# A gated recurrence with a capacity-limited mixture of experts: router logits made pair by pair, softmax sums moved to PSUM, and a new order of work

## The chip, the core and the metric

The kernel runs on one core of a Trainium2 chip. The core has five engines that work side by side, each through its own instructions in the order written: TensorE (PE, with its weight loads shown apart as PEld), VectorE (DVE), ScalarE (ACT), GpSimd (POOL) and SyncE (SP), which here only issues DMA transfers. They wait for each other through semaphores. The metric is the device time of one execution in microseconds; of several runs the median is given.

## What is computed

`x`, `r_gate` and `i_gate` are 4 x 5056 x 256 in float32, 20.7 MB each. The first part is a recurrence over time, the second a mixture of eight experts on its output, where each expert takes only its 80 best tokens:

```python
sig_r, sig_i = sigmoid(r_gate), sigmoid(i_gate)
a_t   = exp(8 * sig_r * log(clip(sigmoid(a_param), 1e-6, 1 - 1e-6)))
x_in  = sqrt(maximum(1 - a_t * a_t, 1e-6)) * sig_i * x
h     = a_t[:, t] * h + x_in[:, t]           # for each t; y[:, t] = h
# the 20224 tokens of y, 256 wide, go on:
logits = y @ w_gate                          # 8 experts
expert = argmax(logits); gate = softmax(logits)[expert]
for e in range(8):                           # 80 tokens at most, by gate
    out[tok] = gate[tok] * (relu(y[tok] @ w1[e]) @ w2[e])   # w1 256x1024, w2 1024x256
# every other row of out is zero
```

So nearly all 20.7 MB of the output are zeros, which the kernel writes by DMA ("zero fills"), and 640 rows are written over them at the end.

## The kernel before

**Tiles.** All 20224 tokens stay on the chip, transposed: `Y` has 25 slots of 128 partitions x 2 halves of the 256 features x 1024 tokens. Slots 0 to 19 end up with the recurrence's states of the 20 "pairs" (stretches of 1024 tokens, the last one 768). The inputs of later pairs pass through slots that are still free, slots 20 to 24 above all. A "unit" is a pair or a part of one: pair 0 is units 0 and 1, pair 19 units 20 and 21.

**Work of a unit**, each step one letter of the table `ORDER`: `r`, `i`, `x` load the inputs (SP, L108); `T` and `I` are the two tanh on ACT (L116, L135); `A` transposes r to PSUM tile `pr` on PE (L122), `E` makes the decay from it on ACT (L124), half by half; `Q` squares it on POOL (L127); `S` takes square roots of several units in one batch on ACT (L131), with a table load on either side; `U` is the product with x on POOL (L138); `B` transposes it to `pu` on PE (L145, L146); `N` is the normalisation on DVE (L149) and `Y` the scan on DVE (L159).

**The router.** Tokens are gated in six "chains": four of 4 pairs, one of 2, and one of the last 1792 tokens. A chain has nine stages, `c0.0` to `c5.8`. Stage 0 makes the logits of the whole chain on PE (L227), 32 float32 matmuls, each two passes in the trace, into one PSUM bank `pl`. Stage 1 copies them out (DVE, L234), 2 turns them (PE, L237, into PSUM bank `pt`), 3 subtracts the maximum (DVE, L241, L242), 4 is the exponential (ACT, L244), 5 finds the first maximum (DVE, L248 to L250), 6 divides by the sum (DVE, L253 to L256; L254 adds 1e-9 to the sums, a tensor_scalar from SBUF to SBUF), 7 turns back (PE, L258) and 8 stores (DVE, L261). In the last chain `l19` and `l20` make the logits of units 19 and 20, and `c5.0` those of unit 21.

**What sets the order.** `ORDER` is a fixed table of such letters, and each engine gets its instructions in that order. `Z` issues one zero fill of 256 tokens (256 KB, in runs of 1 KB, L206) on SP's queue. The fills that are left are written in the program behind the first eight weight loads (`load_w1`, `load_w2` for experts 0 and 1, L295, L298), which reuse slots 20 to 23; some of them are put further ahead in SP's queue by the scheduler.

**After the order**: the choice of 80 tokens per expert (L366 to L438), the gathering of their columns (L509, L510), the matmuls (L524 `ph`, L526 `po`; behind each half of an expert's matmuls the weights of the expert after next are loaded), and the writing of the rows (L537).

Of the kernel before, what the change touches and what calls it, by code (L numbers as in the profile page):

```python
# [63 lines left out]
def moe_kernel(ctx, tc, x, r_gate, i_gate, a_param, w_gate, w1, w2, out, capacity=80):  # L64
# [16 lines left out]
    nc.scalar.dma_start(ap, a_param.rearrange("(h p) -> p h", p=P))  # L81
# [41 lines left out]
    def decay(u, h):  # L123
        nc.scalar.activation(state(u, h), prs.pop((u, h))[:, :UNITS[u][2]], AF.Exp, scale=L[:, h:h + 1], bias=L[:, h:h + 1])  # L124
# [45 lines left out]
    nc.vector.memset(zero, 0.0)  # L170
# [46 lines left out]
    def logits(s, p0, p1, o, n):  # L217

        if 'pl' not in st: st['pl'] = ps_g.tile([P, 512], F32, name="pl")
        c0 = (p0 - CHAINS[s][0]) * PC + o // NR  # L220
        pl = st['pl']
        m = (p1 - p0) * (n // NR)
        for b in range(4):
            for h in range(2):
                for j in range(4):
                    src = Y[:, p0:p1, h, o + 4 * j + b:o + n:NR] if p1 - p0 > 1 else Y[:, p0, h, o + 4 * j + b:o + n:NR]
# [3 lines left out]
    def r_logits(s, n):  # L230
        if s < len(CHAINS) - 1: logits(s, *CHAINS[s], 0, C)
        else: logits(s, UNITS[LASTU][0], UNITS[LASTU][0] + 1, *UNITS[LASTU][1:])
    def r_copy(s, n):
        nc.vector.tensor_copy(lg[:, :count(s)], st['pl'][:, :count(s)])  # L234
    def r_turn(s, n):
        pt = st['pt'] = ps_g.tile([P, 512], F32, name="pt")
        for k in range(nblk(s)): nc.tensor.transpose(pt[:n, k * P:k * P + P], lg[:, k * P:k * P + n], ident)  # L237
    def part(t, s, n, c0=0): return t[:n, c0:c0 + P * nblk(s)].rearrange("p (m e) -> p m e", e=E)
    def r_max(s, n):
        lv = part(st['pt'], s, n)  # L240
# [372 lines left out]
```

## Time and profile before

| | |
|---|---|
| median of 3 runs | 327.68 us (323.89 to 328.71) |
| the profiled execution, and its span | 327.59 us, 325.86 us |
| busy: PE, PEld, DVE, ACT, POOL | 239.6, 201.8, 218.2, 220.8, 202.4 us |
| moved by DMA | 100.77 MB, 309 GB/s over the span |
| chain of waits, largest lines | DVE L159 12%, PE L227 11%, DVE L149 7%, PE L122 7% |

The profile gives for each instruction when it started and how long it took, and, where an engine stood idle before it, for how long and what ended the idle time. Ends of matmuls are modelled, so the sum of their durations says less than the distance from one burst to the next. The chain of waits is followed back from the last instruction to whatever released each step. Stages by time: the ordered part runs to about 246 us, the choice of tokens to 262, the experts to the end.

### The profile page before, as it was taken

Reading aid. Unit: us, or ns where it says so; the run is one execution under the profiler, and the core shown is the slowest. Engines: PE = TensorE matmul, PEld = TensorE weight load, DVE = VectorE, ACT = ScalarE, POOL = GpSimd, SP = SyncE. Lnnn points to the kernel's source line nnn. Section 1 sums busy time; section 2 is a strip of 40 time slices with the busy share of each in tenths; the row PEclk is TensorE's granted clock in tenths of the full one; section 3 lists DMA queues with packets and bytes.
Section 4 is the critical chain, followed back from the end, with each engine's and each line's share of the span. In section 5 each row is a group of like instructions: output and inputs, shape, how many; then the busy total and the mean of one; then the engine's idle time right before and its main releaser. Section 6 shows DMA issues by size and latency. Waiting matters only on the chain.

```text
span 325.9 us, 6481 instructions
## 1 busy us (share of the span) xinstructions
PE 239.6 (74%) x2044; PEld 201.8 (62%) x2044; DVE 218.2 (67%) x467; ACT 220.8 (68%) x399; POOL 202.4 (62%) x289
## 2 busy tenths in 40 slices
PE   0556498689764998676994996394625688999993
PEld 0345498664763757676474935274414478999992
DVE  1000459994999949999769569998718657566420
ACT  4999979999886949999769769547002365445400
POOL 2239998999795957989747570925003466563612
PEclk9999879999998799997999699676575789999999
DMA  6999999999999899979949998909999404999941
GB/s 230 409 412 410 410 355 367 415 406 412 380 383 292 325 362 322 406 257 396 325 161 335 344 315 335 333 20 368 331 363 376 160 2 164 332 339 345 333 111 28
DMA packets 51673, 100.77 MB, mean 309 GB/s; under 512 B 3504, under 2 KB 32048, under 8 KB 51632
## 3 DMA queue, kind: packets, MB, share of 16 engines
q1 hardware_dynamic: 50976, 99.63, 85.1%
q0 software_dynamic: 384, 0.66, 0.6%
q8 instruction: 18, 0.29, 0.4%
q14 instruction: 23, 0.19, 0.2%
q10 hardware_dynamic: 272, 0.00, 0.0%
HBM read 78.91 MB, written 21.36 MB: 308 GB/s over the span
## 4 chain that ended last, share of the span: by engine, by line
PE 31%; DVE 28%; issue 14%; ACT 10%; POOL 8%; DMA 5%; POOLq 3%; DVEq 0%; ACTq 0%; SPq 0%
DVE Y L159 12%; PE pl L227 11%; DVE pu L149 7%; PE pr L122 7%; PE pu L145 6%; PE pu L146 6%; POOL Y L510 6%; ACT Y L124 4%; ACT Y L131 3%; DVE Y L254 3%; POOLq L503 2%; DMA Y<-in_r_gate_dram 2%; ACT Y L116 1%; DMA tiny<-in_a_param_dram 1%; DMA Y<-in_x_dram 1%
## 5 line engine op out<-in xcount | busy, mean ns | idle before, releaser
L138 POOL TENSOR_TENSOR Y<-Y 128x2048 f32<-128x2048 f32 (+2 forms) x22 | 90.5, 4119 | 18.1 <-ACT Y L135 8.2
L127 POOL TENSOR_TENSOR Y<-Y 128x2048 f32<-128x2048 f32 (+2 forms) x22 | 71.6, 3253 | 41.7 <-ACT Y L124 36.6
L145 PE MATMUL pu<-ident,Y 128*128 128x128 f32 x316 | 83.0, 302 | 19.5 <-DVE Y L159 14.8
L159 DVE TENSOR_TENSOR_SCAN Y<-Y,pu 128x1024 f32<-128x1024 f32 (+8 forms) x50 | 93.2, 1882 | 0.9
L146 PE MATMUL pu<-ident,Y 128*128 128x128 f32 x316 | 81.7, 298 | 1.4 <-POOL Y L138 1.4
L122 PE MATMUL pr<-ident,Y 128*128 128x128 f32 x316 | 52.2, 316 | 33.9 <-ACT Y L124 18.5
L149 DVE SCALAR_TENSOR_TENSOR pu<-Y,pu 128x1024 f32<-128x1024 f32 (+2 forms) x44 | 48.6, 1109 | 42.1 <-ACT Y L131 28.4
L122 PEld LDWEIGHTS pr<-ident,Y 128*128 128x128 f32 x316 | 42.5, 164 | 40.9 <-ACT Y L124 22.9
L145 PEld LDWEIGHTS pu<-ident,Y 128*128 128x128 f32 x316 | 49.4, 156 | 26.4 <-DVE Y L159 15.1
L124 ACT ACTIVATE Y<-pr,tiny 128x1024 f32<-128x1024 f32 (+2 forms) x44 | 49.0, 1115 | 23.0 <-PE pr L122 22.9
L146 PEld LDWEIGHTS pu<-ident,Y 128*128 128x128 f32 x316 | 49.5, 157 | 1.7 <-POOL Y L138 1.7
L526 PE MATMUL po<-Y,rows 128*80 128x128 f32 x256 | 46.5, 274 | 0.0
L524 PE MATMUL ph<-Y 128*128 128x80 f32 x256 | 42.7, 258 | 2.4 <-DVE Y L510 1.4
L116 ACT ACTIVATE Y<-Y 128x2048 f32<-128x2048 f32 (+2 forms) x22 | 38.0, 1730 | 5.9 <-DMA Y<-in_r_gate_dram 5.9
L227 PE MATMUL pl<-Y 128*32 128x256 f32 (+4 forms) x512 | 35.7, 443 | 5.9 <-issue 3.8
L524 PEld LDWEIGHTS ph<-Y 128*128 128x128 f32 x256 | 37.5, 191 | 2.9 <-issue 2.9
L135 ACT ACTIVATE Y<-Y 128x2048 f32<-128x2048 f32 (+2 forms) x22 | 38.0, 1730 | 1.7 <-DMA Y<-in_i_gate_dram 1.6
L131 ACT ACTIVATE Y<-Y 128x2048 f32<-128x2048 f32 (+2 forms) x22 | 37.0, 1731 | 2.5 <-POOL Y L127 2.4
L509 ACT COPY Y<-Y 128x2 f32 x224 | 22.9, 191 | 18.1 <-issue 15.4
L510 POOL COPY Y<-Y 128x2 f32 x192 | 24.5, 200 | 15.5 <-issue 8.6
L227 PEld LDWEIGHTS pl<-Y 128*32 128x32 f32 x512 | 15.0, 131 | 23.8 <-issue 20.4
L526 PEld LDWEIGHTS po<-Y,rows 128*80 128x80 f32 x256 | 28.5, 152 | 0.0
(124 smaller groups left out, 178.1 us busy)
## 6 DMA issues: line engine op xcount, KB each, us to landing
out_dram<-Y SPq DMA_DIRECT2D x79, 256.0 KB, 5.9
Y<-in_r_gate_dram SPq DMA_DIRECT2D x18, 1024.0 KB, 7.9
Y<-in_i_gate_dram SPq DMA_DIRECT2D x18, 1024.0 KB, 10.9
Y<-in_x_dram SPq DMA_DIRECT2D x18, 1024.0 KB, 10.6
Y<-in_moe_w_dram SPq DMA_DIRECT2D x32, 512.0 KB, 5.1
Y<-in_r_gate_dram SPq DMA_DIRECT2D x3, 512.0 KB, 4.0
Y<-in_i_gate_dram SPq DMA_DIRECT2D x3, 512.0 KB, 9.3
Y<-in_x_dram SPq DMA_DIRECT2D x3, 512.0 KB
```

What stands on the lines that cost most here:

```text
L122: nc.tensor.transpose(pr[:, c0:min(n, g + 512):nb], rr[:, at:at + P], ident)
L124: nc.scalar.activation(state(u, h), prs.pop((u, h))[:, :UNITS[u][2]], AF.Exp, scale=L[:, h:h + 1], bias=L[:, h:h + 1])
L127: nc.gpsimd.tensor_tensor(halves('r', u), a, a, op=ALU.mult)
L131: nc.scalar.activation(q, q, AF.Sqrt, scale=-0.25, bias=0.25)
L138: nc.gpsimd.tensor_tensor(i, i, flat('x', u), op=ALU.mult)
L145: nc.tensor.matmul(cols, xx[:, at:at + P], ident, start=True, stop=False, is_transpose=True)
L146: nc.tensor.matmul(cols, ii[:, at:at + P], ident, start=False, stop=True, is_transpose=True)
L149: nc.vector.scalar_tensor_tensor(pu, halves('r', u)[:, h], 0.5e-3, pu, op0=ALU.max, op1=ALU.mult)
L159: nc.vector.tensor_tensor_scan(y[:, s0:s1], y[:, s0:s1], q[:, s0:s1], init, op0=ALU.mult, op1=ALU.add)
L227: nc.tensor.matmul(pl[32 * j:32 * j + 32, c0:c0 + m], gates(h, b), src, start=(b == 0 and h == 0), stop=(b == 3 and h == 1), tile_position ...
L524: nc.tensor.matmul(ph[:, c % (FC // 2)], w1v(e1)[:, h, c * P:c * P + P], XG[:, e1, h], start=(h == 0), stop=(h == 1))
L526: nc.tensor.matmul(po[:, h, :P], h2T[:, c], w2v(e2)[:, c, h * P:h * P + P], start=(c == 0), stop=(c == FC - 1))
```

## The change

1. Logits are made one pair at a time: a letter `l` with the unit's number takes the place of stage 0, so that 32 matmuls of 64 columns are issued per pair instead of 32 of 256 per chain. They go to one of two halves of one bank `pl`, even chains to the first and odd ones to the second. `pt` becomes one lasting tile.
2. The exponential is written to `lg` in SBUF, the keys of the first maximum to `pt`, and the sums, with their addition of 1e-9, to `pt` in PSUM; the turn back goes to `pt` too, so that `pl` is free after its copy.
3. `a_param` is loaded by SP as its first transfer, where ACT's queue did it beside SP's first loads.
4. `Z` issues one fill of 512 tokens (512 KB) in runs of 4 KB, from a zeroed 128 x 1024 piece of slot 19, as long as no decay of pair 19 has been written there; after that it issues two old fills.
5. `ORDER` is a new table: other places for loads, fills, chain stages and root batches (12 instead of 11).

```diff
 ORDER = """
-r0@20 r1@20 i0@21 r2@22 i1@21 T0 r3@23 w T1 A0.0 E0.0 r4@24 I0 A0.1 E0.1 T2 Q0 A1.0 i2@18 E1.0 I1 Z ...
+r0@20 r1@20 i0@21 r2@22 i1@21 T0 x0@23 w A0.0 r3@24 E0.0 T1 A0.1 E0.1 i2@18 I0 Q0 A1.0 E1.0 T2 A1.1 ...
...
-    nc.scalar.dma_start(ap, a_param.rearrange("(h p) -> p h", p=P))
+    nc.sync.dma_start(ap, a_param.rearrange("(h p) -> p h", p=P))
...
     def decay(u, h):
+        if UNITS[u][0] == PAIRS - 1: st['last'] = True
...
-    nc.vector.memset(zero, 0.0)
+    nc.vector.memset(Y[:, PAIRS - 1, 0], 0.0)
...
-    def zero_fill(k):
+    def zero_fill(k, wide=False):
...
+            if wide and N - a >= 512 and not st.get('last'):
+                nz[0] = a + 512
+                nc.sync.dma_start(out[a:a + 512].rearrange("(p b) d -> p (b d)", p=P), Y[:, PAIRS - 1, 0])
+                continue
+            if wide:
+                zero_fill(2)
+                continue
...
-    def logits(s, p0, p1, o, n):
-        if 'pl' not in st: st['pl'] = ps_g.tile([P, 512], F32, name="pl")
+    pl = ps_g.tile([P, 2, 256], F32, name="pl")
+    pt = ps_g.tile([P, 512], F32, name="pt")
+    def logits(u):
+        p, o, n = UNITS[u]
+        if p < 18: o, n = 0, C
...
-                    nc.tensor.matmul(pl[32 * j:32 * j + 32, c0:c0 + m], gates(h, b), src,
+                    nc.tensor.matmul(pl[32 * j:32 * j + 32, s % 2, c0:c0 + n // NR], gates(h, b), Y[:, p, h, o + 4 * j + b:o + n:NR],
...
-        nc.scalar.activation(part(st['pt'], s, n, 2 * P), part(st['pt'], s, n), AF.Exp)
+        nc.scalar.activation(part(lg, s, n), part(pt, s, n), AF.Exp)
...
-        m = NR * nblk(s); key = part(st['pl'], s, n, 2 * P)
+        m = NR * nblk(s); key = part(pt, s, n, 2 * P)
...
-        total = sm[:n, :NR * nblk(s)]
-        nc.vector.tensor_reduce(out=total, in_=part(st['pt'], s, n, 2 * P), op=ALU.add, axis=AX.X)
+        total = pt[:n, :NR * nblk(s)]
+        nc.vector.tensor_reduce(out=total, in_=part(lg, s, n), op=ALU.add, axis=AX.X)
         nc.vector.tensor_scalar_add(total, total, 1e-9)
-        nc.vector.reciprocal(total, total)
+        nc.vector.reciprocal(sm[:n, :NR * nblk(s)], total)
```

The order on three pieces, before and in the change. Line numbers of the change stand up to nine higher for the same step.

PE at the first logits (numbers behind a tile's name tell tiles of one name apart), before:

```order
L146 MATMUL pu_513<-ident_72,Y_70 128x128
L122 MATMUL pr_538<-ident_72,Y_70 128x128 [waits Activation_49]
L122 MATMUL pr_538<-ident_72,Y_70 128x128 x7
L227 MATMUL pl_547<-Y_70 32x256 x32
L145 MATMUL pu_589<-ident_72,Y_70 128x128 [waits DMAHW7_49,DVE_49,PE_49]
L146 MATMUL pu_589<-ident_72,Y_70 128x128 [waits DMAHW5_49,Pool_49]
```

and in the change:

```order
L146 MATMUL pu_369<-ident_72,Y_70 128x128
L147 MATMUL pu_369<-ident_72,Y_70 128x128
L236 MATMUL pl_109<-Y_70 32x64 x32
L146 MATMUL pu_423<-ident_72,Y_70 128x128 [waits DVE_49]
L147 MATMUL pu_423<-ident_72,Y_70 128x128
```

The burst of 32 matmuls that stood behind the states of four pairs is a quarter as wide and serves one pair; the next three bursts of the chain stand further down, between other transposes.

SP from the load of unit 20's x to the expert weights, before:

```order
L108 DMA Y<-in_x_dram 128x1024
L206 DMA out_dram<-Y 256x1x256
L112 DMA Y<-in_i_gate_dram 128x512
L206 DMA out_dram<-Y 256x1x256 x3
L112 DMA Y<-in_x_dram 128x512
L206 DMA out_dram<-Y 256x1x256 x11
L295 DMA Y<-in_moe_w_dram 128x2x512 x4
L298 DMA Y<-in_moe_w_dram 128x4x256 x4
L206 DMA out_dram<-Y 256x1x256 x15
```

and in the change:

```order
L112 DMA Y<-in_i_gate_dram 128x512
L108 DMA Y<-in_x_dram 128x1024
L112 DMA Y<-in_x_dram 128x512
L214 DMA out_dram<-Y 256x1x256 x26
L300 DMA Y<-in_moe_w_dram 128x2x512 x4
L303 DMA Y<-in_moe_w_dram 128x4x256 x4
L214 DMA out_dram<-Y 256x1x256 x30
```

Ahead of this piece SP's queue has 49 fills of 256 KB before, and 11 of 512 KB and one of 256 KB in the change. Behind the load of the last x come 26 fills before and 56 in the change.

PE at the end of the router, before:

```order
L258 MATMUL pl<-ident,lg 128x128 [waits DVE_49]
L227 MATMUL pl<-Y 32x64 [waits DVE_49]
L227 MATMUL pl<-Y 32x64 x31
L227 MATMUL pl<-Y 32x32 x32
L227 MATMUL pl<-Y 32x16 x4
L227 MATMUL pl<-Y 32x16 [waits DVE_49]
L227 MATMUL pl<-Y 32x16 x27
L237 MATMUL pt<-ident,lg 112x128 [waits DVE_49]
L258 MATMUL pl<-ident,lg 128x112 [waits DVE_49]
```

and in the change:

```order
L236 MATMUL pl<-Y 32x32 x32
L236 MATMUL pl<-Y 32x16 [waits DVE_49]
L236 MATMUL pl<-Y 32x16 x3
L236 MATMUL pl<-Y 32x16 [waits DVE_49]
L236 MATMUL pl<-Y 32x16 x27
L263 MATMUL pt<-ident,lg 128x128 [waits DVE_49]
L242 MATMUL pt<-ident,lg 112x128 [waits DVE_49,Activation_49]
L263 MATMUL pt<-ident,lg 128x112 [waits DVE_49]
```

Unit 19's logits have moved ahead of the last transposes, and chain 4's turn back (the 128x128 one) now comes behind the last logits instead of ahead of unit 19's.

## Rows read from the trace of the kernel before

**Rows 1.** Busy time by window: PE, PEld, DVE, ACT, POOL, clock, DMA share, GB/s.

```profile
0.00:218.00 218.00, 160.07 (x1248) 128.93 (x1249) 157.02 (x149) 182.67 (x132) 158.45 (x62) 0.92 0.92 340
218.00:234.00 16.00, 8.22 (x40) 6.20 (x38) 14.12 (x22) 7.22 (x10) 4.81 (x4) 0.65 0.97 323
234.00:246.00 12.00, 4.56 (x194) 3.84 (x194) 3.45 (x12) 0.25 (x1) 0.29 (x1) 0.64 1.04 351
```

**Rows 2.** Groups by line and shape, 0 to 246 us: busy, mean ns | idle before.

```profile
L227 PE MATMUL pl<-Y 128*32 128x256 f32 x256 | 28.3, 607 | 0.0
...
L227 PE MATMUL pl<-Y 128*32 128x64 f32 x64 | 2.0, 291 | 1.1 <-DVE rows L261 1.1
...
L227 PE MATMUL pl<-Y 128*32 128x16 f32 x64 | 1.0, 194 | 3.8 <-issue 3.8
```

**Rows 3.** Timeline of DVE: start, duration, [idle before <- what ended it].

```profile
79.65 0.42 DVE L234 COPY lg<-pl 128x256 f32<-128x256 f32 x1 [2.71 <-PE pl L227]
...
118.90 0.42 DVE L234 COPY lg<-pl 128x256 f32<-128x256 f32 x1 [4.34 <-PE pl L227]
...
165.97 1.23 DVE L149 SCALAR_TENSOR_TENSOR pu<-Y,pu 128x1024 f32<-128x1024 f32 x1 [3.24 <-PE pu L146]
...
194.94 0.42 DVE L234 COPY lg<-pl 128x256 f32<-128x256 f32 x1 [2.76 <-PE pl L227]
```

**Rows 4.** Timeline of ACT, behind three bursts of logits.

```profile
119.90 1.21 ACT L124 ACTIVATE Y<-pr,tiny 128x1024 f32<-128x1024 f32 x1 [4.42 <-PE pr L122]
...
166.78 1.21 ACT L124 ACTIVATE Y<-pr,tiny 128x1024 f32<-128x1024 f32 x1 [2.73 <-PE pr L122]
...
219.31 0.56 ACT L124 ACTIVATE Y<-pr,tiny 128x256 f32<-128x256 f32 x1 [4.05 <-PE pr L122]
```

**Rows 5.** Chain of waits: start, length, what; the pieces on L254.

```profile
97.98 3.65 DVE Y L254
...
148.44 1.18 DVE Y L254
...
204.65 3.05 DVE Y L254
```

**Rows 6.** Who waited for whom, 60 to 234 us: total, times, longest.

```profile
PEld pl L258 <- DVE lg L256: 9.3, 4, 3.2
...
ACT Y L116 <- DMA Y<-in_r_gate_dram: 5.9, 5, 3.0
```

**Rows 7.** Timeline of all engines near the start.

```profile
0.81 0.87 SPq L108 DMA_DIRECT2D Y<-in_r_gate_dram  x2
...
5.59 0.17 DVE L87 TENSOR_SCALAR tiny<-tiny 128x2 f32<-128x2 f32 x1 [4.26 <-DMA tiny<-in_a_param_dram]
...
7.54 2.00 ACT L116 ACTIVATE Y<-Y 128x1024 f32<-128x1024 f32 x2
...
26.73 1.90 ACT L135 ACTIVATE Y<-Y 128x2048 f32<-128x2048 f32 x1
```

**Rows 8.** DMA issues of 0 to 9 us: count, KB each, median us to landing.

```profile
Y<-in_r_gate_dram SPq DMA_DIRECT2D x2, 512.0 KB, 4.3
```

**Rows 9.** Groups of the whole span: the table loads around root batches.

```profile
L131 ACT ACT_TABLE_LOAD x11 | 14.1, 1283 | 0.2
```

**Rows 10.** Timeline of the end of the router.

```profile
241.74 0.27 DVE L234 COPY lg<-pl 128x112 f32<-128x112 f32 x1 [6.96 <-PE pl L227]
...
244.75 0.18 DVE L254 TENSOR_SCALAR Y<-Y 112x16 f32<-112x16 f32 x1
```

**Rows 11.** Timeline of SP's queue, from the load of unit 20's x.

```profile
218.25 0.33 SPq L108 DMA_DIRECT2D Y<-in_x_dram  x1
...
239.34 14.93 SPq L206 DMA_DIRECT2D out_dram<-Y  x15
268.10 6.77 SPq L295 DMA_DIRECT2D Y<-in_moe_w_dram  x3
```

**Rows 12.** Timeline of PE, where the third expert's matmuls begin.

```profile
277.76 0.35 PE L524 MATMUL ph<-Y 128*128 128x80 f32 x2
```

More of the change, by code (lines that the diff above doesn't have):

```diff
@@ L50 @@
+B19.0 I20 E20.0 t B19.1 S19.1 A20.1 x20@21 l18 x21@21 Z Z Z Z E20.1 T21 Q20 N19.0 Z A21.0 E21.0 N19.1 I21 Z A21.1 U20 E21.1 Y19.0 Z Q21
+S20.2 Z Y19.1 B20.0 U21 Z N20.0 B20.1 Z c4.1 Y20.0 l19 Z N20.1 B21.0 Y20.1 c4.2 Z N21.0 B21.1 c4.3 Z l20 N21.1 c4.4 Y21.0 Y21.1 c4.5 l21
+c4.6 c4.7 c5.1 c4.8 c5.2 c5.3 c5.4 c5.5 c5.6 c5.7 c5.8
 """
@@ L216, in gates @@
     def gates(h, b): return wg[:, h, 24 - E * b:56 - E * b]
-    def logits(s, p0, p1, o, n):
-        if 'pl' not in st: st['pl'] = ps_g.tile([P, 512], F32, name="pl")
-        c0 = (p0 - CHAINS[s][0]) * PC + o // NR
-        pl = st['pl']
-        m = (p1 - p0) * (n // NR)
+    pl = ps_g.tile([P, 2, 256], F32, name="pl")
[3 more added lines that the diff above has]
+        if p < 18: o, n = 0, C
+        s = next(k for k, c in enumerate(CHAINS) if p < c[1])
+        c0 = (p - CHAINS[s][0]) * PC + o // NR
         for b in range(4):
@@ L225, in logits @@
                 for j in range(4):
[L226 to L227 removed]
+                    nc.tensor.matmul(pl[32 * j:32 * j + 32, s % 2, c0:c0 + n // NR], gates(h, b), Y[:, p, h, o + 4 * j + b:o + n:NR],
                                      start=(b == 0 and h == 0), stop=(b == 3 and h == 1), tile_position=(0, 32 * j))
     def by_expert(v, n, s): return v[:n, :NR * nblk(s)].unsqueeze(2).broadcast_to([n, NR * nblk(s), E])
[L230 to L232 removed]
     def r_copy(s, n):
[L234 removed]
+        nc.vector.tensor_copy(lg[:, :count(s)], pl[:, s % 2, :count(s)])
     def r_turn(s, n):
[L236 removed]
         for k in range(nblk(s)): nc.tensor.transpose(pt[:n, k * P:k * P + P], lg[:, k * P:k * P + n], ident)
@@ L239, in r_max @@
     def r_max(s, n):
-        lv = part(st['pt'], s, n)
+        lv = part(pt, s, n)
         nc.vector.tensor_reduce(out=mx[:n, :NR * nblk(s)], in_=lv, op=ALU.max, axis=AX.X)
@@ L251, in r_gate_ @@
     def r_gate_(s, n):
-        total = sm[:n, :NR * nblk(s)]
-        nc.vector.tensor_reduce(out=total, in_=part(st['pt'], s, n, 2 * P), op=ALU.add, axis=AX.X)
+        total = pt[:n, :NR * nblk(s)]
+        nc.vector.tensor_reduce(out=total, in_=part(lg, s, n), op=ALU.add, axis=AX.X)
         nc.vector.tensor_scalar_add(total, total, 1e-9)
-        nc.vector.reciprocal(total, total)
-        nc.vector.tensor_tensor(part(lg, s, n, 2 * P), part(st['pl'], s, n, 2 * P), by_expert(sm, n, s), op=ALU.mult)
+        nc.vector.reciprocal(sm[:n, :NR * nblk(s)], total)
+        nc.vector.tensor_tensor(part(lg, s, n, 2 * P), part(pt, s, n, 2 * P), by_expert(sm, n, s), op=ALU.mult)
     def r_back(s, n):
-        for k in range(nblk(s)): nc.tensor.transpose(st['pl'][:, k * P:k * P + n], lg[:n, (2 + k) * P:(3 + k) * P], ident[:n, :n])
+        for k in range(nblk(s)): nc.tensor.transpose(pt[:, k * P:k * P + n], lg[:n, (2 + k) * P:(3 + k) * P], ident[:n, :n])
     def r_store(s, n):
         c0 = CHAINS[s][0] * PC + (K1 if s >= EARLY else 0)
-        nc.vector.tensor_copy(rows[:, c0:c0 + count(s)], st.pop('pl')[:, :count(s)])
-    stages = (r_logits, r_copy, r_turn, r_max, r_exp, r_first, r_gate_, r_back, r_store)
+        nc.vector.tensor_copy(rows[:, c0:c0 + count(s)], pt[:, :count(s)])
+    stages = (None, r_copy, r_turn, r_max, r_exp, r_first, r_gate_, r_back, r_store)
     def top16(src, val, idx, tmp):
@@ L277, in moe_kernel @@
              'B': u_transposes, 'N': normed, 'Y': scan, 'c': lambda s, k: stages[k](s, width(s)), 't': early_top,
-             'l': lambda u: logits(len(CHAINS) - 1, UNITS[u][0], UNITS[u][0] + 1, *UNITS[u][1:]), 'Z': lambda: zero_fill(1), 'w': gate_weights}
+             'l': logits, 'Z': lambda: zero_fill(1, True), 'w': gate_weights}
     with tc.manual_schedule(engines={E_.Activation, E_.PE, E_.DVE, E_.Pool, E_.SP}):
```

35 lines of the change are left out of this document (16 added, 19 removed).

## The prediction

> **What bounds the kernel now.** I read the busy times by window first, to see which engine could end the ordered part earlier. Up to 234 us, where the last scan is done, ACT works 182.7 + 7.2 = 189.9 us, DVE 171.1, POOL 163.3, and the DMA engines are busy 92% and 97% of the time [rows 1]. No engine is full: ACT has 44 us idle. So this part is bound by how the engines wait for each other in their fixed orders, with DMA close behind. Then I read the groups and timelines for what ends the idle times. Four chains make their logits in bursts of 28.3/4 = 7.1 us each on PE [rows 2], and nothing else passes PE meanwhile. DVE stands idle behind each of the four, 2.71 + 4.34 + 3.24 + 2.76 = 13.1 us together [rows 3]; ACT stands idle behind two of them and behind the shorter burst of chain 4, 4.42 + 2.73 + 4.05 = 11.2 us [rows 4]. The chain of waits shows a second loss: the addition of 1e-9 to 16 or 32 numbers per partition (L254) takes 3.65, 1.18 and 3.05 us in three chains [rows 5], and 0.18 in the last one, where POOL does next to nothing [rows 1, 10]. Last I read SP's queue behind the ordered part: it ends its fills at 254.3 us and has nothing to issue until 268.1 [rows 11]. That idle time is the cover of part 7.
>
> **The change part by part.** The sum is made against the profiled execution, 327.6 us, which is 0.1 under the median of 327.7.
>
> 1. *Start.* `a_param` lands at 5.56 and the first tanh starts at 7.54, 1.95 us behind DVE's first use of it [rows 7]. r's first load goes out at 0.81 and lands 4.3 us later, at 5.1 [rows 7, 8]; SP spends 0.87/2 = 0.43 on an issue, so behind `a_param` it lands at 5.5. If `a_param` lands by 3.6, the tanh starts at 5.5, a gain of 2.0. If it needs the 4.3 of the row, it lands at 5.1 and the gain is 0.5. I take 2.0, since the row's 4.3 carries 512 KB and this load 1 KB. The DMA page of the Trainium skill (DMA: Bandwidth & Descriptors, Anatomy of one DMA) puts the fixed part of a transfer at about 2 us; by that estimate it lands at 2.8 and r's load decides, which no row here shows. Ahead of the first root batch the new order has one i-tanh less on ACT, 1.9 us [rows 7], but the first decay directly behind the first tanh, so that ACT waits for four transposes, where the second tanh (1.0 us) covered them: about 1.3. Together -2.6, between -0.5 and -3.
>
> 2. *Logits pair by pair.* PE does the same work: a pair needs 64 passes of 64 columns, 2.0 us in the only row of that shape, in a window whose granted clock averaged 0.64, and a quarter of 7.1 is 1.8 [rows 1, 2]. Twenty pairs make 35 to 40 us against 36 before. What falls is the longest stretch in which transposes wait, from 7.1 to 1.9, by 73%. At best all DVE idle behind bursts goes, -13; at worst nothing, if other waits stand behind it. I take 73% of ACT's 11.2, -8.2, because ACT has the most work and must run ahead of DVE. No logits wait in PE's queue for a scan of their own pair except the last two units': PE has only two `pu` buffers, and the logits stand behind the transposes that need the earlier ones free.
>
> 3. *Sums in PSUM.* The three long additions shrink from 7.9 to three times 0.18, -7.3 on DVE [rows 5, 10]. On another engine's time this gives only what waited for DVE; I take a third, -2.5, between 0 and -7.3. The row shows an addition of the same width between 0.18 and 3.65. The SBUF page of the Trainium skill (SBUF — State Buffer, Who interferes with whom) says that a tensor_scalar in a two-port mode and GpSimd wait for each other's whole instruction; the VectorE page (VectorE: DVE Perf Modes, Why PSUM operands drop a tier) says that an operand in PSUM rules that mode out. Against the change, its errata section gives a PSUM source 120 cycles of fixed time against 58, an estimate of 0.065 us more in two instructions of six chains, 0.8 us in all; by it the term would be -1.7. No row has such an instruction. The exponential's new target, the wide memset and the cast are hidden beside POOL's and PE's work; without that cover they cost under 1 us once.
>
> 4. *Fills.* Ahead of the last loads SP's queue carried 49 to 53 fills and now the bytes of 23: 30 x 0.262 = 7.9 MB less, at 340 GB/s 23 us of DMA time [rows 1]. This time is mostly not on the path, since loads wait for slots. What it can give is ACT's waits for r, 5.9 us in five [rows 6]. I take -3, between 0 and -5.9. The longer runs add little: they touch only 22 of 79 fills.
>
> 5. *Order.* One more root batch is two more table loads, 2 x 1.283 = +2.6 on ACT [rows 9]. What else the new order makes wait can't be read from rows; its bound is rival B.
>
> 6. *End of the router.* DVE idles 6.96 us behind the last scan, until three units' logits are made, of which 3.8 is a pause of PE for nothing that is shown [rows 2, 10]. Now only the last 16 columns' passes are left, 1.0 us, and seven short DVE steps of chain 4 (0.2 to 0.4 each, some 2.1) stand in that gap, then its turn back (about 0.9). Without the pause the gain is 4; with it some 1.2. I take -2.5.
>
> 7. *Fills behind the last load.* Here the change adds. Between the load of unit 20's x and the weights of the third expert SP now has 56 fills, eight weight loads and the last two loads: 14.7 + 4.2 + 0.8 = 19.7 MB, at 351 GB/s 56 us [rows 1]. Before, those weights were asked for 49.9 us behind that load [rows 11], now 2.5 less, 47.4: 8.7 late. They are used 277.76 - 268.10 = 9.7 us after that [rows 11, 12], and landing takes 4.3 of these if nothing is ahead [rows 8], or 1.5 if the queue hides its start. So PE waits 0.5 to 3.3 us; I take +2. At 323 GB/s [rows 1] it is some 5 us more, so 0 to +8. Behind this everything is paced by PE's matmuls.
>
> Sum: -2.6 - 8.2 - 2.5 - 3 + 2.6 - 2.5 + 2 = -14.2, and 327.6 - 14.2 = **313.4 us**.
>
> **The rivals.** *B, the gain is taken back:* the new order has waits of its own that fill what bursts, additions and fills left, and only start, end and the fills behind the last load remain: -2.6 - 2.5 + 2, 324.5 us. For it: ACT's 44 us of idle time end in many short waits, of which the named ones are less than half, and late pairs have only slots 20 to 24 to load into. Against it: the three losses are long single pieces. *C, the addition still waits* in its PSUM form (the change does not do what it says): without -2.5, 315.9. For it: rows show only the SBUF form. Against it: no other DVE instruction of the chains varies like that. *D, slower:* the stages of neighbouring chains now share `pt`, and turn and turn back stand in PE's queue waiting for DVE. Before, such waits cost PE's weight loads 9.3 us in four, 3.2 the longest [rows 6]. If the ten of chains 0 to 4 cost 3.2 each, that is 22.7 more, 336.1 us; from 2.35 on average the gain of 14.2 is gone. For it: more steps between two users of one bank. Against it: in most places of the new order several transposes stand between DVE's step and PE's.
>
> **How the numbers follow.** My forecast has a chance of 0.64, C 0.06, B 0.21, D 0.09. The upper end takes in B, and part 7 with 8 instead of 2 on a middling gain; all bounds at their best would give 297, but ACT's own 192.5 us of work and its start keep the ordered part from that, so the lower end is 303. That leaves D and the far ends out: 303 to 325. A measurement of this kernel tells about 2% from no change, that is 321.1 to 334.2. Faster than that: forecast and C, less a tenth that lands above, and a quarter of B, 0.69; within 0.22; slower 0.09.
>
> **What the changed kernel's profile would show.** Part 1: first tanh at 5.5. Part 2: no idle of DVE or ACT over 2 us that a logits row ends, and the last scan done near 221. Part 3: all additions of the sums under 0.3 us. Part 4: no waits of ACT for r after 60 us. Part 6: DVE idle under 3 us behind the last scan. Part 7: DMA busy without a gap between choice and third expert, and PE waiting there for weights by 0 to 3 us. The forecast is wrong if ACT's idle time ahead of the last scan stays near 44 us (then B), or if PE's waits ended by DVE at the turns pass 23 us (D).

## The result and the profile after

The changed kernel takes 309.08 us (median of 4 runs, 307.61 to 313.03), before 326.25 (323.89 to 328.71): a ratio of 0.946, 95% interval 0.935 to 0.957. An execution more than 1.5% above the fastest of its kernel counts as slow, and ratios, here and below, leave those out where medians do not. Predicted were 313.4 us, between 303 and 325, a fall of 14.2; measured are 17.2 by the medians. The total is right, but two of its terms are not: the ordered part gives more than I summed, and a loss that I had priced at 2 us, and put down to another mechanism, takes part of it back.

The profiled execution took 313.0 us, the longest of the four; a second profile, of an execution of 308.3 us (the first experiment), stands beside it where the two differ. Where each stage ends, in us, read from the rows named (start plus duration for the first two):

| stage ends with | before | after | second profile |
|---|---|---|---|
| last scan (DVE L160, before L159) | 234.78 | 213.79 | 212.51 |
| router's last store (DVE L266, before L261) | 246.35 | 221.19 | 219.69 |
| start of 14 matmuls on tile `pd` ahead of the experts (PE L347, before L342) | 259.92 | 234.97 | 233.18 |
| first matmul of two experts side by side (PE L531, before L526) | 271.48 | 254.62 | 250.04 |
| span | 325.9 | 311.2 | 306.5 |

Each row less the one above it: the scans end 21.0 us earlier (22.3 in the second profile), the router's end is 4.2 (4.4) shorter, the choice is unchanged, the stretch into the experts is 8.1 (5.3) longer, and the rest 2.2 (2.0) longer. The 14 matmuls on `pd` make nothing that is used; the kernel has them there only to keep PE busy (`keep_warm`). The expectations below call them transposes.

**The start.** The timeline of all engines, as in [rows 7]:

```profile
0.81 0.43 SPq L81 DMA_DIRECT2D tiny<-in_a_param_dram  x1
...
2.94 0.17 DVE L87 TENSOR_SCALAR tiny<-tiny 128x2 f32<-128x2 f32 x1 [0.82 <-DMA tiny<-in_a_param_dram]
...
5.01 1.06 ACT L116 ACTIVATE Y<-Y 128x1024 f32<-128x1024 f32 x1
...
7.29 0.78 ACT L125 ACTIVATE Y<-pr,tiny 128x512 f32<-128x512 f32 x1 [1.22 <-PE pr L122]
```

The first tanh starts at 5.01 in place of 7.54; 5.5 was forecast. The 1 KB of `a_param` is used 2.13 us behind its issue; by the fixed 2 us of the Trainium skill (DMA: Bandwidth & Descriptors, Anatomy of one DMA) I had estimated that it lands at 2.8. That section is on transfers that GpSimd issues, and this one is SP's; its 2.13 us are near that figure. ACT then waits 1.22 us for four transposes (1.3 expected).

**The ordered part.** Busy times by window (PE, PEld, DVE, ACT, POOL, clock, DMA share, GB/s), as in [rows 1]:

```profile
0.00:198.00 198.00, 158.08 (x2088) 142.68 (x2088) 149.37 (x146) 182.33 (x132) 156.70 (x61) 0.96 0.93 348
198.00:214.00 16.00, 9.76 (x188) 7.68 (x188) 14.32 (x18) 9.66 (x13) 6.62 (x5) 0.79 1.03 351
```

ACT did 189.9 us of work in 234 before; now it does 192.0 in 214, and 182.3 in the first 198. Its idle time is 22 us where it was 44. Who waited for whom, 60 to 221 us (total, times, longest), beside [rows 6]:

```profile
PEld pt L263 <- DVE lg L261: 5.0, 2, 3.5
...
ACT Y L125 <- DMA Y<-in_r_gate_dram: 2.2, 1, 2.2
ACT Y L116 <- DMA Y<-in_r_gate_dram: 1.5, 1, 1.5
PEld pt L242 <- DVE lg L240: 1.0, 1, 1.0
...
ACT Y L125 <- PE pr L122: 0.8, 2, 0.5
```

ACT's waits for transposes have all but gone (0.8 us in two; [rows 4] had three of 2.7 to 4.4), and no idle time of DVE or ACT above 2 us is ended by a row of logits. ACT still waits 3.7 us for r, where the forecast had none behind 60 us. PE's waits for DVE at the turns are 6.0 us (9.3 in [rows 6]): rival D does not show. The groups of 0 to 221 us have the logits and the table loads of the root batches, as [rows 2, 9] had them:

```profile
L236 PE MATMUL pl<-Y 128*32 128x64 f32 (+2 forms) x1344 | 39.1, 280 | 0.8 <-DVE Y L160 0.8
...
L132 ACT ACT_TABLE_LOAD x12 | 15.4, 1283 | 0.2
```

The logits take PE as long as forecast (39.1 us, 35 to 40), and one batch more loads its tables; all of ACT's table loads together are 26, before 24. On DVE's timeline the additions of 1e-9 in the four long chains ([rows 5]) are all like this one:

```profile
109.68 0.20 DVE L259 TENSOR_SCALAR pt<-pt 128x32 f32<-128x32 f32 x1
```

**The router's end.** DVE's timeline, as in [rows 10]; the 6.96 us of idle time are gone:

```profile
212.41 1.38 DVE L160 TENSOR_TENSOR_SCAN Y<-Y,pu 128x256 f32<-128x256 f32 x2
...
215.71 0.27 DVE L240 COPY lg<-pl 128x112 f32<-128x112 f32 x1
```

**The way into the experts** is where time is lost. The timeline of all engines there:

```profile
222.38 27.23 SPq L214 DMA_DIRECT2D out_dram<-Y  x30
...
234.97 5.68 PE L347 MATMUL pd<-Y,ident 128*128 128x256 f32 x14
...
241.12 3.12 POOL L515 COPY Y<-Y 128x2 f32 x24 [8.38 <-PE pd L347]
241.88 2.75 ACT L514 COPY Y<-Y 128x2 f32 x28 [11.06 <-issue]
241.93 3.15 DVE L515 COPY Y<-Y 128x2 f32 x27 [6.29 <-issue]
...
245.92 7.09 PE L529 MATMUL ph<-Y 128*128 128x80 f32 x32 [5.26 <-DVE lg L549]
...
250.63 3.26 DVE L515 COPY Y<-Y 128x2 f32 x28 [4.97 <-issue]
```

DVE's copies of the first two experts' columns before:

```profile
262.09 3.15 DVE L510 COPY Y<-Y 128x2 f32 x27 [2.13 <-issue]
...
267.70 3.26 DVE L510 COPY Y<-Y 128x2 f32 x28 [1.87 <-issue]
```

They stood behind 2.13 and 1.87 us of "issue", time in which the engine waited for nothing that the profile shows. Now it is 6.29 and 4.97, and ACT and POOL start no earlier than DVE's. SP issues fills until 249.6, beside the copies, where before it had issued the last one by 254.3, ahead of all copies ([rows 11]). PE then makes its first 32 matmuls in 7.09 us and goes on at a low clock, as the busy times by window (columns as above) show:

```profile
246.00:254.60 8.60, 7.46 (x34) 7.27 (x35) 3.26 (x28) 3.07 (x29) 3.84 (x31) 0.50 0.76 246
254.60:260.40 5.80, 5.80 (x32) 5.80 (x32) 4.07 (x34) 1.54 (x15) 4.50 (x36) 0.51 0.25 91
260.40:311.20 50.80, 45.69 (x450) 45.46 (x448) 21.60 (x155) 18.10 (x161) 20.60 (x111) 0.97 0.75 244
```

The granted clock is 0.50 and 0.51, the lower of its two levels (1.2 of 2.4 GHz), up to 260.4, behind an idle time of 5.26 us. The clock had come up to 1.00 in 240 to 242 us, at the end of the 14 matmuls on `pd`, and was back at 0.50 in 244 to 246, so the wait lost what those matmuls had gained. No row of PE waits for weights. So part 7's loss is there, but not as late weights.

### The profile page after: what moved, and what is told of

Its sections match the earlier page's. It is cut to its first block, busy times and chain, and to the rows that moved or that the text cites. A ratio compares the mean times of both kernels' runs of the same rounds, so it can differ in the third digit from the quotient of the medians.

```text
span 311.2 us, 8151 instructions
## 1 busy us (share of the span) xinstructions
PE 243.6 (78%) x2876; PEld 220.9 (71%) x2876; DVE 211.7 (68%) x467; ACT 222.7 (72%) x401; POOL 202.9 (65%) x289
## 4 chain that ended last, share of the span: by engine, by line
issue 24%; POOL 22%; ACT 13%; DVE 13%; PE 12%; DMA 11%; POOLq 4%; SPq 0%; DVEq 0%; ACTq 0%
POOL Y L128 9%; POOL Y L515 6%; DMA Y<-in_x_dram 5%; POOL Y L139 5%; ACT Y L125 5%; DVE Y L160 4%; PE pr L122 4%; DMA Y<-in_i_gate_dram 4%; ACT Y L132 4%; POOLq L508 3%; DVE pu L150 3%; PE pu L147 3%; PE pu L146 3%; ACT Y L116 2%; ACT L125 2%
## 5 line engine op out<-in xcount | busy, mean ns | idle before, releaser
L160 DVE TENSOR_TENSOR_SCAN Y<-Y,pu 128x1024 f32<-128x1024 f32 (+8 forms) x50 | 93.4, 1882 | 0.9
L146 PE MATMUL pu<-ident,Y 128*128 128x128 f32 x316 | 78.0, 289 | 9.2 <-DVE Y L160 7.7
L147 PE MATMUL pu<-ident,Y 128*128 128x128 f32 x316 | 77.3, 287 | 4.3 <-POOL Y L139 4.3
L122 PE MATMUL pr<-ident,Y 128*128 128x128 f32 x316 | 51.4, 312 | 31.1 <-ACT Y L125 19.1
L122 PEld LDWEIGHTS pr<-ident,Y 128*128 128x128 f32 x316 | 40.9, 161 | 39.3 <-ACT Y L125 27.3
L146 PEld LDWEIGHTS pu<-ident,Y 128*128 128x128 f32 x316 | 47.0, 149 | 13.2 <-DVE Y L160 9.1
L529 PE MATMUL ph<-Y 128*128 128x80 f32 x256 | 47.7, 284 | 6.4 <-DVE lg L549 5.3
L147 PEld LDWEIGHTS pu<-ident,Y 128*128 128x128 f32 x316 | 47.0, 149 | 5.5 <-POOL Y L139 5.5
L531 PE MATMUL po<-Y,rows 128*80 128x128 f32 x256 | 48.4, 282 | 0.0
L529 PEld LDWEIGHTS ph<-Y 128*128 128x128 f32 x256 | 42.7, 218 | 7.0 <-issue 7.0
L236 PE MATMUL pl<-Y 128*32 128x64 f32 (+2 forms) x1344 | 39.1, 280 | 0.8 <-DVE Y L160 0.8
L236 PEld LDWEIGHTS pl<-Y 128*32 128x32 f32 x1344 | 33.9, 124 | 4.4 <-issue 3.3
L515 DVE COPY Y<-Y 128x2 f32 x224 | 24.7, 178 | 11.6 <-issue 11.6
```

The lines of the kernel that those rows point to most:

```text
L122: nc.tensor.transpose(pr[:, c0:min(n, g + 512):nb], rr[:, at:at + P], ident)
L146: nc.tensor.matmul(cols, xx[:, at:at + P], ident, start=True, stop=False, is_transpose=True)
L147: nc.tensor.matmul(cols, ii[:, at:at + P], ident, start=False, stop=True, is_transpose=True)
L160: nc.vector.tensor_tensor_scan(y[:, s0:s1], y[:, s0:s1], q[:, s0:s1], init, op0=ALU.mult, op1=ALU.add)
L236: nc.tensor.matmul(pl[32 * j:32 * j + 32, s % 2, c0:c0 + n // NR], gates(h, b), Y[:, p, h, o + 4 * j + b:o + n:NR], start=(b == 0 and h == ...
L515: else: eng.tensor_copy(dst, src)
```

## The experiments

Each was timed beside runs of the kernel before on its chip; ratios are to those, with 95% intervals.

| run | median us | ratio to before | last scan | stretch into experts |
|---|---|---|---|---|
| changed kernel again | 309.73 | 0.953 [0.947, 0.959] | 212.51 | 16.9 |
| late fills left out | 300.99 | 0.924 [0.919, 0.929] | 212.25 | 11.8 |
| late fills from DRAM | 307.92 | 0.945 [0.940, 0.951] | 212.26 | 11.7 |
| six fills in the gaps | 309.64 | 0.952 [0.947, 0.957] | 214.97 | 17.3 |
| logits in bursts | 333.88 | 1.023 [1.016, 1.030] | 237.55 | 16.5 |
| sums in SBUF | 313.50 | 0.962 [0.956, 0.968] | 219.64 | 18.9 |
| a_param on ACT | 312.06 | 0.959 [0.953, 0.964] | 214.99 | 18.9 |
| new forms, old table | 327.31 | 1.004 [0.997, 1.010] | 234.40 | 11.6 |
| fills in 1 KB runs | 310.27 | 0.949 [0.945, 0.954] | 212.52 | 19.9 |
| gaps, fills copied | 301.68 | 0.925 [0.922, 0.929] | 215.16 | 11.7 |
| old table, logits spread | 320.68 | 0.974 [0.967, 0.981] | 229.39 | 11.6 |
| four gaps, fills copied | 301.93 | 0.928 [0.925, 0.931] | 211.53 | 11.7 |

The last two columns are from each run's one profile, in us: the end of the last scan, and from the start of the matmuls on `pd` to the first matmul of two experts (11.6 before). Five profiles of kernels that differ only behind the router or in the fills' runs (the changed kernel's two, and runs 2, 3 and 9) have the last scan at 212.25 to 213.79, so a difference of some 1.5 us in that column says nothing. Line numbers of one step differ by up to five between runs.

**1. The changed kernel again**, no edit.

> The changed kernel once more, unaltered, as the base of the other three and for a second profile. Its profiled execution took 313.0 us where its other runs took 307.6 to 309.6, and of its 19.2 us from the transposes that keep PE busy ahead of the experts (start 234.97) to the first matmuls of two experts side by side (254.15), before had 11.3 (259.92 to 271.22). My theory S: these 7.9 us are lost in the copies of the experts' columns, where all three copying engines stand idle for nothing shown, 11.1, 6.3 and 5.2 us at the longest, while SP's 30 fills run until 249.6; it expects the stretch at 17 to 20 us again and a time of 307 to 310. Rival K: the loss is PE's half clock in that one profile (7.1 us for the first 32 matmuls where before needed 3.8, and 0.78 us per pair of steps up to 260.4 where 0.40 follow); it expects a stretch of 13 to 15 us in an execution of 308 us.

The stretch is 16.9 us in an execution of 308.3, and 16.4 to the matmul that the expectation counts to: under S's 17, over K's 15, so this run alone does not decide. PE's first 32 matmuls took 5.89 us behind an idle time of 3.93. In both profiles PE stands idle again behind them (1.14 us for DVE's copies in the changed kernel's, 1.65 here), so the low clock did not set the end of the stretch; DVE's waits of 4.68 and 4.18 us ahead of its copies did. That speaks for S.

**2. The late fills left out.**

```
-    zero_fill(-(-N // ZERO_TOKENS))
```

> The 30 fills behind the first weight loads are left out (their rows of the output stay unwritten). S: the copying engines resume as in before, the stretch from the transposes to the first matmuls of two experts is 11 to 12 us, and the time falls by 6 to 11 us against the changed kernel, to 298 to 302. K, or any cause within the engines: no change, within 2 us. The prediction's part 7, in which the fills cost by making the third expert's weights late: the first matmuls of two experts stay where they are and only PE's wait for weights goes, which in the changed kernel's profile is 0, so no change either.

As S has it: 8.7 us less by the medians, and the stretch as short as before (11.8 us). The same stretch of the timeline:

```profile
235.45 3.15 DVE L514 COPY Y<-Y 128x2 f32 x27 [2.17 <-issue]
...
239.44 3.77 PE L528 MATMUL ph<-Y 128*128 128x80 f32 x32 [0.76 <-DVE lg L548]
```

DVE's idle times are back at 2.17 us and, ahead of the second expert's copies, 1.87, and PE, which waits only 0.76, takes 3.77 at a clock of 1.00. K, or any cause within the engines, had expected no change.

**3. The late fills from DRAM.** In `zero_fill`, for the late ones only:

```
-  nc.sync.dma_start(out[a:b]..., zero.unsqueeze(1).broadcast_to([P, m, ZC]))
+  nc.sync.dma_start(out[a:b]..., x[0, a % 4096:a % 4096 + b - a]...)
```

> The 30 late fills keep their place, size and run length, but copy rows of x from DRAM to the output, where they read the zeroed tile in SBUF (so these rows hold x). It parts two forms of S. S1: what the engines wait for is a read of SBUF (each column number is read into a register before its copy), which stands behind the fills' own reads of SBUF; then the stall goes, with 11 to 13 us in the stretch and 4 to 8 us less in all. S2: the engines wait for something that itself comes through the full DMA engines (their own instructions; the DMA view of the changed kernel shows an instruction transfer in 241 to 246 and two in 246 to 248); then the stall stays at 17 to 20 us, or grows, since such a copy loads DRAM twice.

The same stretch:

```profile
223.89 24.62 SPq L215 DMA_DIRECT2D out_dram<-in_x_dram  x30
...
235.16 3.15 DVE L519 COPY Y<-Y 128x2 f32 x27 [2.16 <-issue]
```

S2 is out. SP issues until 248.5, the DMA engines are as busy as in the changed kernel (a share of 1.03 to 1.07 in 232 to 238 us, 1.09 in the changed kernel's stretch), and yet DVE stands for 2.16 and 1.87 us as with no fills at all. So a full queue alone does not hold the engines. One thing besides the source changed with the edit, though: how the bytes are cut. In the changed kernel (234 to 256 us) and here (232 to 246):

```profile
DMA packets 6882, 7.17 MB, mean 326 GB/s; under 512 B 401, under 2 KB 6388, under 8 KB 6879
...
DMA packets 595, 4.87 MB, mean 348 GB/s; under 512 B 297, under 2 KB 297, under 8 KB 297
```

The copies go in far fewer and larger packets, so the number of small ones was a rival. The kernel before answers it: while it loads weights into SBUF, in 276 to 300 us, small packets are many and the rate is the same, and ACT, which by the code reads column numbers there too, waits 1.42 us, no more than the 1.61 of run 2, where nearly nothing is moved:

```profile
DMA packets 5922, 8.01 MB, mean 334 GB/s; under 512 B 272, under 2 KB 3904, under 8 KB 5915
...
290.67 1.42 ACT L509 COPY Y<-Y 128x2 f32 x14 [1.42 <-issue]
```

What is left, as far as these runs part it, is that the fills read SBUF. That the held work is the reads of column numbers is inferred: by the code these are what the three engines do there, but the trace does not show them. The total falls by only 1.8 us, where S1 had 4 to 8, since now part 7's own mechanism appears (waits, 221 to 306 us):

```profile
PE ph L533 <- DMA Y<-in_moe_w_dram: 4.3, 1, 4.3
```

**4. Six fills more in the gaps**, 18 late ones left.

```
-x10@12 Y6.1 ... i11@16 T11 ... x14@24
+x10@12 Z Z Y6.1 ... i11@16 Z Z Z T11 ... x14@24 Z
```

> Six wide fills more in the ordered part, at places where SP waits for a slot and the DMA engines are not full (share 0.84 in 80 to 90 us, 0.49 in 90 to 100, 0.89 in 120 to 130), so 18 late fills in place of 30. 12 x 0.262 MB is 3.1 MB, at 370 GB/s 8.5 us: the fills end near 241. S: the first stall stays in part, the second goes, and the time falls by 3 to 7 us to 302 to 306, if the loads of 88 to 135 us do not become late. Rival: the ordered part, 94% full of DMA, gives it all back (the last scan 3 to 6 us later), and the time stays within 2 us. K: no gain, 0 to 3 us slower.

No gain by the medians, as the rival has it. DVE's second stall goes and the first stays, as its timeline shows:

```profile
241.87 3.03 DVE L515 COPY Y<-Y 128x2 f32 x26 [5.91 <-issue]
...
247.47 3.29 DVE L515 COPY Y<-Y 128x2 f32 x28 [1.87 <-issue]
```

The stretch is no shorter for that, 17.3 us: PE, which had waited 5.15, takes 7.45 us for its first 34 matmuls and goes on without a pause, so here the low clock sets the end. The last scan is 2.5 us later than the second profile's, in an execution 1.7 us above its run's median.

**5. Logits in bursts again**, here chain 0; the others likewise.

```
-l1 N3.0 ... A7.0 l2 r11@24 ... Q7 l3 N5.1 T10 Y5.1 l4 x9@14
+N3.0 ... A7.0 r11@24 ... Q7 N5.1 T10 Y5.1 l1 l2 l3 l4 x9@14
```

> The changed kernel with the logits of a chain made in one burst again: each l is moved behind, to the place of the last l of its chain, so that 128 matmuls of 64 columns stand together (64 for chain 4); all else stays. The prediction's part 2 expects its 8.2 us back (0 to 13), about 318 against the changed kernel's 309.7, with idle times of 3 to 4 us of DVE or ACT behind each burst. Rival O: the gain lies in the new table as a whole, in which ACT is busy 182.3 of the first 198 us and runs far enough ahead that a burst of 7 us is absorbed; then 0 to 2 us more, 310 to 312.

Both were wrong: it costs 24 us by the medians (7.0%, 23 us, by the ratios), three times my term, and the new table's ratio to the old kernel is 1.023. ACT's timeline behind two of the bursts:

```profile
169.66 1.21 ACT L125 ACTIVATE Y<-pr,tiny 128x1024 f32<-128x1024 f32 x1 [8.30 <-PE pr L122]
...
202.47 1.20 ACT L125 ACTIVATE Y<-pr,tiny 128x1024 f32<-128x1024 f32 x1 [7.91 <-PE pr L122]
```

DVE's, behind all four:

```profile
82.27 1.23 DVE L150 SCALAR_TENSOR_TENSOR pu<-Y,pu 128x1024 f32<-128x1024 f32 x1 [8.26 <-PE pu L147]
...
124.71 0.42 DVE L240 COPY lg<-pl 128x256 f32<-128x256 f32 x1 [6.09 <-PE pl L236]
...
168.86 1.23 DVE L150 SCALAR_TENSOR_TENSOR pu<-Y,pu 128x1024 f32<-128x1024 f32 x1 [9.99 <-PE pu L147]
...
201.45 0.42 DVE L240 COPY lg<-pl 128x256 f32<-128x256 f32 x1 [8.99 <-PE pl L236]
```

PE's timeline of the third burst:

```profile
155.02 3.96 PE L236 MATMUL pl<-Y 128*32 128x64 f32 x136
...
161.26 3.50 PE L236 MATMUL pl<-Y 128*32 128x64 f32 x120 [2.29 <-issue]
```

DVE idles 33.3 us behind the four bursts, ACT 20.5 behind three (4.30 behind the second). A burst of the new form is longer than the old 7.1 us: this one lasts 9.7 us, with a pause of PE that nothing in the trace explains.

**6. The sums in SBUF again.**

```
-        total = pt[:n, :NR * nblk(s)]
+        total = sm[:n, :NR * nblk(s)]
```

> The changed kernel with the softmax sums, and their addition of 1e-9, in SBUF again (sm in place of pt); all else stays. The prediction's part 3: the additions take 1 to 3.7 us again in two or three chains, and 2.5 us come back (0 to 7.3), 312. Rival: with PSUM elsewhere the addition costs the same 0.2 us, or its 3 us fall on a DVE with slack: no change within 1 us.

DVE's timeline, the additions of three chains:

```profile
108.96 3.73 DVE L259 TENSOR_SCALAR Y<-Y 128x32 f32<-128x32 f32 x1
...
149.59 1.76 DVE L259 TENSOR_SCALAR Y<-Y 128x32 f32<-128x32 f32 x1
...
174.26 4.26 DVE L259 TENSOR_SCALAR Y<-Y 128x32 f32<-128x32 f32 x1
```

and POOL's, beside the first and the third:

```profile
108.06 4.59 POOL L139 TENSOR_TENSOR Y<-Y 128x2048 f32<-128x2048 f32 x1
...
173.95 4.53 POOL L139 TENSOR_TENSOR Y<-Y 128x2048 f32<-128x2048 f32 x1
```

The three additions take 9.75 us where they took 0.60, and the kernel 3.8 us more by the medians; the ratios differ by 0.9% (2.9 us), just beyond what their intervals leave open. The outcome is that of the rule of the Trainium skill weighed in part 3 (SBUF — State Buffer, Who interferes with whom), and the trace agrees: the first addition ends at 112.69 and POOL's instruction at 112.65, the third at 178.52 and 178.48, the second 0.04 behind POOL's square in the same way. The fourth, which started while POOL stood idle, took 0.18. In the changed kernel the addition at 109.68 runs in 0.20 us in the middle of POOL's product. The last scan in the table, 219.64, is of an execution 4.2 us above the median.

**7. `a_param` on ACT's queue again.**

```
-    nc.sync.dma_start(ap, a_param...)
+    nc.scalar.dma_start(ap, a_param...)
```

> The changed kernel with a_param on ACT's queue again. The first tanh started at 5.01 us in the changed kernel's profile and at 7.54 before; here it starts at 7.0 to 7.6 again. The prediction's part 1 expects 2.0 us back, 311.7. Rival: the head start is absorbed by waits for loads before the end of the ordered part, no change within 0.7 us.

ACT's timeline:

```profile
7.26 1.06 ACT L116 ACTIVATE Y<-Y 128x1024 f32<-128x1024 f32 x1
```

The first tanh starts at 7.26, 2.25 us later, and the last scan ends 2.5 later. The ratios differ by 0.6% (1.9 us), which these intervals don't part from nothing; the profile and the size agree with the term, but a gain in the total is not shown.

**8. The new forms in the old table**: `ORDER` is the old one, with `l1 l2 l3 l4` for `c0.0` and so on, and `Z` one fill of 256 tokens.

> The new forms in the old table: logits by pair but all four at the old place of stage 0, sums in PSUM, a_param first, one lasting pt, and fills of 256 tokens at the old places (65 ahead of the weights, 14 behind, as the table gives). So a_param and the sums alone, without the spread of the logits and without the new order. The prediction's terms give 2.0 + 2.5 us for these, 327.6 - 4.5 = 323, and up to 1.3 more at the router's end. Rival O (the table as a whole) expects the same 321 to 325, and differs from the prediction in the burst run only. Rival D in its small form (stages of neighbouring chains wait for one another in pt, where the old table leaves few steps between them): 326 to 332.

327.3 us, no gain, where the terms gave 323, though the additions take 0.20 us here too. DVE's waits, 40 to 230 us:

```profile
DVE lg L240 <- PE pl L236: 16.8, 3, 7.6
```

Behind three of the bursts DVE idles 16.8 us where the same three of [rows 3] had 9.8. The longer bursts are what stands against the gains of the sums and the start; that they eat them exactly is not shown. Rival D's time fits, but its mechanism does not show: PE's weight loads wait 5.9 us for DVE at the turns, fewer than the 9.3 of [rows 6].

**9. Fills in 1 KB runs**: `Z` issues two fills of 256 tokens.

> The changed kernel with two fills of 256 tokens in runs of 1 KB wherever it issues one of 512 tokens in runs of 4 KB: the same bytes at the same places. The prediction costed the longer runs at nothing, as they touch 22 of 79 fills: no change, within 1 us. Rival: the ordered part, where the DMA engines are busy 94% of the time, gains from them; then 2 to 5 us slower, 312 to 315, with a later last scan.

No difference; the longer runs are worth nothing here, as costed.

**10. Gaps, and late fills copied from zeroed rows of the output.**

```
+  src = out[:b - a]...
-  nc.sync.dma_start(out[a:b]..., zero...)
+  nc.sync.dma_start(out[a:b]..., src if late else zero...)
```

> The run with six fills more in the gaps, and its 18 late fills made by copying rows of the output that were zeroed before, in place of reading the zeroed tile in SBUF, so that the output is whole. S1 (reads of column numbers wait behind the fills' reads of SBUF): the stretch from the transposes to the first matmuls of two experts falls from 19 to 11 to 13 us; the ordered part stays 1.5 to 2.5 us later; the third expert's weights, asked for near 242 in place of 249.5, come in time: 302 to 305. Rival W: copies load DRAM twice, the weights of the third expert come late, as in the run with 30 copies where PE waited 4.3 us for them: 306 to 310.

The same stretch once more:

```profile
237.67 3.03 DVE L516 COPY Y<-Y 128x2 f32 x26 [2.17 <-issue]
```

S1 again, in a kernel that computes the whole output: 301.7 us, 8 less than the changed one, a little under S1's range, and PE waits for no weights.

**11. The old table with the logits spread**: `l1` behind `Y2.1`, `l2` behind `Y3.1`, and so on.

> The new forms in the old table, as in the run that took 327.3 us, but with the logits of 14 pairs spread: each l stands right behind the last scan of the pair after its own, the others at the old place of stage 0. The prediction's part 2, 8.2 us for the spread whatever the table: 319 (314 to 327). The burst run lost 24 us in the new table; if the spread is worth that in any table, 303 to 308. Rival T: the spread pays only where the table gives ACT and the loads their head start, so that other waits of the old table stand behind it: 324 to 328.

6.6 us less than run 8 by the medians, 2.9% (9.5 us) by the ratios, of which this run's rests on only two of its six executions. Here the spread is worth about the 8.2 of the prediction.

**12. Four gaps, fills copied**: as run 10, with `x10@12 Z` and none behind `x14@24`.

> As the run with gaps and copies, but with four wide fills more and not six: one behind the load at 82 us, three behind the one at 88.4, where SP stands idle for 6 and 8 us, and none at 119 to 127. So 22 late copies. If the sixth and fifth fill were what made the ordered part later in the gap run (last scan 1.2 to 2.9 us later), it is as early as in the changed kernel here, 211 to 213; the fills end some 3 us later than with six. S1: 301 to 305. W: 306 to 310.

The ordered part is as early as in the changed kernel (211.53), and the total that of run 10. In the profiles the 2.5 us of runs 4 and 10 go with the two fills left out here, one behind the load at 82 us and one at 119 to 127. Those were executions 1.7 and 1.9 us above their medians, though, and the totals show no difference.

## Why the prediction was right, and where not

**Part 1, start (-2.6): right by the profiles.** The tanh is 2.5 us earlier; run 7 takes 2.25 of that back and the last scan follows. In the total the difference is within the intervals.

**Part 2, pair by pair (-8.2): the mechanism holds, the size fits only the old table.** There it measured 5 us at the last scan and 6.6 to 9.5 in the total. In the new table it is worth 23 to 24. Ends of the last scan with the new forms, each of one execution, show it as a square: old table, bursts 234.40; old table, spread 229.39; new table, bursts 237.55; new table, spread 212.51. The table alone loses 3 us, the spread alone gains 5, both together gain 22. The ratios, 1.004, 0.974, 1.023 and 0.953, say the same of the total, which carries the later loss in the new table: 6 us lost, 9.5 gained, 16 gained together. ACT's waits for transposes, from the start to the last scan, make the same square; the kernel before, then the four in that order:

```profile
ACT Y L124 <- PE pr L122: 22.9, 21, 4.4
...
ACT Y L125 <- PE pr L122: 24.4, 20, 6.9
...
ACT Y L125 <- PE pr L122: 14.4, 17, 2.3
...
ACT Y L125 <- PE pr L122: 29.4, 19, 8.3
...
ACT Y L125 <- PE pr L122: 5.1, 10, 1.2
```

ACT works 190 to 192.5 us in each; its whole idle time is 44, 39, 45 and 21 us in the four. I had taken 73% of ACT's waits behind bursts as they stood in the trace of before, as if the rest of the order stayed.

**Part 3, sums (-2.5): right**, 2.9 to 3.8 us, some 30 to 40% of the 9.2 that DVE saves; I had taken a third. The 0.8 us estimated against the change do not show: undisturbed, the addition takes 0.20 us in PSUM and 0.18 in SBUF, and the reciprocal 0.36 from PSUM and 0.35 from SBUF.

**Parts 4 and 5, fills and order (-3 and +2.6): the mis-sized step.** The two more table loads are there, and ACT's waits for r fell by 2.2 us ([rows 6]: 5.9, now 3.7). But the sentence "What else the new order makes wait can't be read from rows; its bound is rival B" bounded the order on the bad side only. From run 11 to the second profile the last scan moves by 16.9 us (the total by 11 by the medians, as only the new table loses time on the way into the experts), of which I had -0.4 in the sum. What shows in its place is ACT's waits: 9.3 us less for transposes and 6 less for the loads of r and i. Which of the table's moves does it (loads, fills, root batches or stages) was not tested one by one, and that cause stays open. Of the fills, run 9 shows that their run length is not it, and run 12 that four wide ones more in the ordered part move the last scan by nothing.

**Part 6, router's end (-2.5): right in place, 4.2 us**, the value it had "without the pause"; PE's pause of 3.8 us does not come again there.

**Part 7, fills behind the last load (+2): the loss is real, its mechanism was not the one in force.** Weights of the third expert were not waited for. The stretch grew by 8.1 us in the profiled execution and 5.3 in the second, and 2 us more went behind it at a low clock. As far as the runs show, the fills did it by reading SBUF while the engines read their column numbers from it (runs 2, 3, 10). Late weights come next: with that stall removed and the queue as long, PE waited 4.3 us for them (run 3).

That the sum of 14.2 us lies so near the 14.7 between the two spans, or the 17.2 of the medians, is luck: 7.3 more came from the ordered part (21.0 against 13.7) and 1.7 from the router's end, and 8.5 more were lost behind it (10.5 against 2). With the second profile the spans are 19.4 apart. Rivals B, C and D are out: ACT's idle time fell to 22 us, every addition took 0.2, and the turns cost 6.0. Two slips in the working change nothing of this: the chance of "faster" adds up to 0.68 and not 0.69, and the 0.18 us of [rows 10] is an addition half as wide as those of [rows 5]; one of their width, at 182.88 us of the trace before, took 0.18 too.

## What to carry to other kernels

Where two edits act on the same queue, price them as a square and not as a sum, in other words each alone and both together: here the new order was worth nothing until the long bursts were out of its way. When an early stage gets faster, list what used to be over by the time the next stage begins; here it was a run of zero fills, and it met work that had never been beside it. Ask of a background transfer not only how many bytes it moves but which memory it reads: copying the late zero fills from DRAM rows was worth 8 us here (run 10 against run 4).

## What the hardware showed

- Ahead of their first copies ACT, POOL and DVE stood 11.06, 8.38 and 6.29 us while fills read SBUF, 5.96, 4.32 and 2.17 with no fills (run 2), and 5.96, 4.32 and 2.16 with as busy a queue fed from DRAM (run 3).
- PE's clock went with its waits in all 14 profiles: the first 32 matmuls of the experts took 3.77 us behind an idle time of 0.21 to 1.36, and 5.7 to 7.1 behind 3.4 to 5.5 us, with a granted clock of 1.00 in run 2 and 0.50 in the changed kernel. The order within the long ones is not strict: 5.89 behind 3.93, 7.09 behind 3.43 (run 7).
- An addition of a number in SBUF by DVE, 0.18 us alone, ended 0.04 us behind POOL's instruction in each of three cases in which it started beside one (run 6), and the same addition in PSUM took 0.20 beside POOL.
- 256 matmuls of 64 columns in a row do not run as four times the 1.96 us of 64: PE paused once in each of the four bursts of run 5, for 1.5 to 2.3 us, and the trace does not say for what.
